# Splitting the first F tiles of a fused S5-scan and MLP kernel by token parity, with zeroed warm-up matmuls and later waits for weights

## The chip, the cores and the metric

The kernel runs on one core of one Trainium2 chip. The metric is the device time of one launch in microseconds (us). The engines are named as the profile names them: PE (TensorE, matmuls; PEld is its weight load), DVE (VectorE), ACT (ScalarE), POOL (GpSimd) and SP (SyncE, which here only issues DMAs). Each engine works through its own queue in order, and engines wait for one another by semaphores.

## What is computed

The input is x with 2048 tokens of 448 values. It is normalised, and two things are made of the normalised xn: a diagonal complex state-space scan (S5) and a gated two-layer MLP. In short:

```python
xn = layernorm(x)
Lam_bar = exp(dt * Lam);  B_bar = ((Lam_bar - 1) / Lam)[:, None] * Bmat
h[t] = Lam_bar * h[t-1] + xn[t] @ B_bar.T            # 448 complex states
s = 2 * real(h @ Cmat.T) + xn * Dskip
m = gelu(layernorm(xn) @ w1 + b1) @ w2 + b2          # w1: 448 x 1792, w2: 1792 x 448
out = x + s * silu(m)
```

## The kernel before, in words

Tokens are taken in four groups of 512 (`g`), each of two blocks of 256 tokens (`b`). Two neighbouring tokens share a partition, so that a block is 128 partitions by two token parities (`par`, or `r` in the layout). `xn2T` holds the normalised tokens transposed, with 128 columns for one block and parity.

**The order of the work is written out by hand.** Every operation, or run of operations on one engine, is a task (`Plan.add`, line 64) with the names that it reads and writes. `Plan.link` (line 93) works out which task waits for which. `Plan.emit` (line 112) then goes through the list `ORDER` (line 161) and issues each task on its engine, with all its waits ahead of its first instruction. The tasks are numbered in the order in which the code makes them; a few have names (W0 to W3, B0 to B3, H10, H12 and so on). `SECOND` (line 181) lists the tasks that go to their second choice of engine. An engine never overtakes: a task whose wait isn't met holds up all that stand behind it on that engine.

**The head.** The first block is normalised parity by parity (`first_norm`, line 386): statistics on DVE (393, 394), the root on ACT (395, 396), the scaling on DVE (398, tasks 92 and 99), four transposes on PE (401, tasks 93 and 100), and a copy back from PSUM on DVE (405, tasks 95 and 102). After each four transposes stand five dummy matmuls (403, tasks 94 and 101). Ahead of all that, task 88 (line 828) has PE run 28 dummy matmuls of the identity with itself, which need the identity that POOL makes. Task 45 (lines 480 to 485) is nine tiny matmuls that turn the rows of scan parameters into columns; ACT copies them out (46, the last parameter row for the skip in 47), takes an exponential (48, 54), and POOL computes with them (53, 49 to 52, 55, 56), until ACT takes the absolute value of an angle (task 57, line 512) and POOL goes on with a sine (58).

**The first layer for group 0** (`mm1_half`, line 742) takes 128 x 2 tokens at a time. For each of the seven pairs `j` of F tiles it runs 8 matmuls of 128 weights columns by 256 tokens (both parities at once, 4 slices of D by 2 tiles) into a pair of PSUM banks, and then one gelu on ACT (line 754). The pairs of banks are taken in turn, 0 and 1, 2 and 3, 4 and 5, so the matmuls of a pair wait for the gelu of three pairs earlier. For block 0 the matmul tasks are 114, 116, 118, 120, 122, 124 and 126, and their gelus 115, 117, 119, 121, 123, 125 and 127; for block 1 they are 128 to 141. Task 112 (line 464) is the eight transposes of block 1, and 113 (line 470) their copy. Each first-layer task waits for its chunk of w1: rows 0 to 383 (`w1_c`), the last 64 rows (`w1r_c`), and the row of b1 that stands below them (`w1b`).

**The second layer** (`mm2`, line 758) is 14 matmuls of 128x448 for 128 tokens. The four tasks of group 0 (275, 272, 281, 278) each wait for all four chunks of w2. Then PE goes on with the first layer of group 1 (`mm1`, line 720: an `own` task of 8 matmuls, which has the name H1j, and an `other` task of 6 for each `j`, bank pairs 0 and 1, 2 and 3, 5 and 6), whose gelus on ACT (line 738) are 365 for j = 0, 369 for j = 2, 367 for j = 1. H15 (j = 5) takes the banks that H12 (j = 2) used, so it waits for gelu task 369.

**ACT between the gelus of groups 0 and 1.** ACT multiplies the B matrices, which a DMA brings, by parameters (167 and 169, line 595), copies rows of w1 (W1, W2, W3, line 843; W0 is on DVE, line 844), loads another function table (581), makes the sines and cosines for the scan (579, tasks 162 to 166), takes three silus (766), loads the gelu table again, and goes on with 365. `ln_apply` for the scan's normalised tokens of block 0 is tasks 146 and 147 (one a parity), of block 1 148 and 149; on ACT they are line 449, on DVE line 448. W1 waits for W0.

## Time and profile before

| what | value |
|---|---|
| median of 3 runs | 155.54 us (155.49 to 155.61) |
| the profiled execution's own time | 155.18 us |
| its span, first to last instruction | 153.1 us |
| PE busy | 148.4 us, 97% of the span |
| DVE, ACT, POOL busy | 131.3, 102.5 and 47.3 us |
| granted TensorE clock | 1.000 |

The span is what the profile sees; 2.1 us of the profiled execution's own time lie around it. Busy time counts instructions from their start to their end, and since matmuls overlap in the PE's pipeline, a matmul's duration is longer than the distance to the next one. A row of a timeline gives start, length, engine, line, operation, what is written and read, and how many instructions were merged; a bracket tells the idle time just ahead and what ended it. "q" after an engine is its sequencer, as when SP issues a DMA.

### The profile page before, as it was taken

What the parts mean: (1) busy time and instruction counts of PE and PEld (TensorE: products, weight loads), DVE (VectorE), ACT (ScalarE), POOL (GpSimd) and SP (SyncE); (2) the same over time, 40 slices, a digit from 0 to 9 for tenths busy, and PEclk for the clock granted to TensorE, in tenths of its full rate; (3) what the DMA queues carried; (4) which work ended last, traced back from release to release, by engine and by line L of the source; (5) the groups of instructions that cost most, each with busy time, mean ns of one, the idle gap of its engine ahead of it and who ended that gap; (6) DMA issues with size and microseconds to landing.
All of it is one profiled execution on the core that took longest, in us unless ns stands there. A gap on an engine that the chain in (4) does not pass through costs nothing.

```text
span 153.1 us, 3017 instructions
## 1 busy us (share of the span) xinstructions
PE 148.4 (97%) x1079; PEld 89.9 (59%) x1079; DVE 131.3 (86%) x275; ACT 102.5 (67%) x175; POOL 47.3 (31%) x122
## 2 busy tenths in 40 slices
PE   6999999999999999999999999999999999999992
PEld 6899945454575555755544556665555665555551
DVE  5879999999988999999859998349699539999784
ACT  3876959999885688798993599841419987244110
POOL 6465896374520004700000079000512920000001
PEclk9999999999999999999999999999999999999999
DMA  4998999996859553000003310042300100010103
GB/s 115 311 259 268 349 175 238 211 187 130 160 88 175 88 103 69 0 2 0 4 1 59 84 40 0 0 96 84 62 2 0 62 0 4 0 62 0 60 0 120
DMA packets 31512, 14.04 MB, mean 92 GB/s; under 512 B 25733, under 2 KB 31113, under 8 KB 31498
## 3 DMA queue, kind: packets, MB, share of 16 engines
q1 hardware_dynamic: 31344, 13.80, 39.5%
q8 instruction: 8, 0.13, 0.4%
q10 hardware_dynamic: 154, 0.06, 0.1%
q14 instruction: 6, 0.05, 0.1%
HBM read 6.20 MB, written 1.84 MB: 53 GB/s over the span
## 4 chain that ended last, share of the span: by engine, by line
PE 85%; SPq 6%; DMA 5%; issue 1%; DVE 1%
PE psum L762 28%; PE psum L728 22%; PE psum L654 15%; PE psum L792 13%; SPq L90 6%; DMA w_sb<-in_B_w_dram 5%; PE psum L795 4%; PE psum L636 3%; PE psum L798 1%; PE psum L642 1%; DVE t L801 0%; DVE tmp L804 0%; PE psum L638 0%; PE psum L644 0%
## 5 line engine op out<-in xcount | busy, mean ns | idle before, releaser
L762 PE MATMUL psum<-w_sb,gT 128*128 128x448 bf16 x224 | 44.3, 353 | 0.1
L728 PE MATMUL psum<-xn2T,w_sb 64*128 64x512 bf16 x294 | 33.9, 378 | 0.0
L762 PEld LDWEIGHTS psum<-w_sb,gT 128*128 128x128 bf16 x224 | 21.8, 98 | 19.8 <-DMA w_sb<-in_B_w_dram 0.4
L738 ACT ACTIVATE gT<-psum,b1f 128x512 bf16<-128x512 f32 x42 | 26.0, 687 | 6.9 <-PE psum L728 6.7
L728 PEld LDWEIGHTS psum<-xn2T,w_sb 64*128 64x128 bf16 x294 | 15.6, 109 | 16.1 <-issue 3.0
L654 PE MATMUL psum<-xnT,BT 128*128 128x256 bf16 x196 | 24.1, 273 | 0.0
L654 PEld LDWEIGHTS psum<-xnT,BT 128*128 128x128 bf16 x196 | 18.4, 98 | 6.5 <-issue 3.3
L766 ACT ACTIVATE g_sb<-o 128x448 bf16<-128x448 f32 x16 | 9.1, 572 | 12.2 <-DVE o L765 12.1
L801 DVE TENSOR_TENSOR t<-psum,g_sb 128x448 bf16<-128x448 f32 (+2 forms) x17 | 10.0, 591 | 5.9 <-PE psum L795 2.8
L679 DVE TENSOR_TENSOR_SCAN s_f<-cw,cur,v_sb 128x256 f32<-128x256 f32 x21 | 14.9, 737 | 0.1
L693 POOL TENSOR_TENSOR cwk<-s_f,ang 128x3 f32<-128x3 f32 x3 | 1.4, 470 | 43.3 <-DVE s_f L679 43.3
L748 PE MATMUL psum<-xn2T,w_sb 128*128 128x256 bf16 x112 | 12.6, 273 | 0.3 <-DVE xn2T L405 0.3
L748 PEld LDWEIGHTS psum<-xn2T,w_sb 128*128 128x128 bf16 x112 | 11.9, 111 | 0.7 <-issue 0.4
L792 PE MATMUL psum<-CZ,h_sb 128*128 128x448 bf16 x56 | 11.9, 353 | 0.0
L765 DVE TENSOR_TENSOR o<-psum,b2bc 128x448 f32<-128x448 f32 x16 | 9.7, 614 | 1.7 <-PE psum L762 1.7
L792 PE MATMUL psum<-CQ,h_sb 128*128 128x448 bf16 (+2 forms) x54 | 10.5, 332 | 0.0
L683 ACT ACTIVATE s_b<-s_f 128x1536 bf16<-128x1536 f32 x4 | 5.9, 1485 | 6.7 <-DVE s_f L679 6.7
L658 ACT ACTIVATE u_sb<-psum 128x512 bf16<-128x512 f32 x12 | 7.2, 598 | 4.6 <-PE psum L654 4.6
L448 DVE TENSOR_SCALAR xn_sb<-x_all,lnw 128x448 bf16<-128x448 bf16 (+1 forms) x30 | 9.9, 364 | 0.3
L754 ACT ACTIVATE gT<-psum 128x512 bf16<-128x512 f32 x14 | 8.2, 592 | 2.7 <-PE psum L748 2.7
L804 POOL TENSOR_TENSOR tmp<-t,xr 128x192 bf16<-128x192 bf16 x1 | 0.5, 548 | 26.3 <-DVE t L801 26.3
L792 PEld LDWEIGHTS psum<-CZ,h_sb 128*128 128x128 bf16 x56 | 5.3, 98 | 5.1 <-issue 0.5
(160 smaller groups left out, 236.9 us busy)
## 6 DMA issues: line engine op xcount, KB each, us to landing
out_dram<-tmp SPq DMA_DIRECT2D x7, 224.0 KB, 1.9
x_all<-in_A_x_dram SPq DMA_DIRECT2D x3, 448.0 KB, 4.7
w_sb<-in_B_w_dram SPq DMA_DIRECT2D x3, 448.0 KB, 7.3
w_sb<-in_B_w_dram SPq DMA_DIRECT2D x3, 384.0 KB, 4.4
Bn<-in_A_B_im_dram SPq DMA_DIRECT2D x1, 336.0 KB, 8.5
Bn<-in_A_B_re_dram SPq DMA_DIRECT2D x1, 336.0 KB, 8.7
x_all<-in_A_x_dram SPq DMA_DIRECT2D x2, 112.0 KB, 2.1
x_all<-in_A_x_dram SPq DMA_DIRECT2D x1, 224.0 KB, 2.7
```

The source lines that it names most:

```text
L90: return e.dma_start(out_ap, in_ap)
L448: on = [("dve", [lambda e, o=o, i=i: e.tensor_scalar(o, i, rs, nb, op0=ALU.mult, op1=ALU.add) for o, i in pairs], 0.4, 0.12), ("act", [lam ...
L654: fns = [lambda e, r=r, m=m, d=d: e.matmul(psum[:, 4, r * NK:(r + 1) * NK], BT[:, m, d, :], xnT[:, gx, d, :], start=(d == 0), stop=(d == 6 ...
L679: dve(lambda e, i=i, ri=ri, init=init: e.tensor_tensor_scan(s_f[:, i, ri, :], col(R2, i).to_broadcast([128, NK]), v_sb[:, i, ri, :], init, ...
L728: return lambda e: e.matmul(psum[:, b0 + k, :], w1_sb[halves[h], d, fcol(2 * j + k)], rhs[halves[h], d, :, :], start=first and d == 0, sto ...
L738: act([lambda e, k=k: e.activation(gT[:, gb, 2 * j + k, :], psum[:, b0 + k, :], ACT.Gelu_apprx_tanh, bias=b1f[:, 2 * j + k:2 * j + k + 1]) ...
L748: fns = [lambda e, k=k, d=d: e.matmul(psum[:, banks[k], :].rearrange("p (r c) -> p r c", r=2)[:, :, cs], w1_sb[:, d, fcol(2 * j + k)], rhs ...
L762: fns = [lambda e, fi=fi: e.matmul(psum[:, bk, 0:D], gT[:, gb, fi, q * 128:(q + 1) * 128], w2_sb[:, fi, :], start=(fi == 0), stop=(fi == N ...
L765: dve(lambda e: e.tensor_tensor(o2[:, ob, :], psum[:, bk, 0:D], b2bc[:], ALU.add), [f"ps{bk}", "b2bc"], [f"oo{ob}"], 0.62, prio - 76)
L766: act(lambda e: e.activation(g_sb[:, gs, :], o2[:, ob, :], ACT.Silu), [f"oo{ob}"] + (["silu"] if g == 0 else []), [f"g{gs}"], 0.58, prio - ...
L792: fns = [lambda e, k=k: e.matmul(psum[:, bk, c0:c1], h_sb[:, hb, k, k0:k0 + 128], cm[:, k, c0:c1], start=(k == 0), stop=False) for k in ra ...
L801: dve(lambda e: e.tensor_tensor(t3[:, fb, c0:c1], psum[:, bk, c0:c1], g_sb[:, gs, c0:c1], ALU.mult), [f"ps{bk}", f"g{gs}"], [f"t3{fb}_{c0} ...
```

## The change

- **First F tiles by parity.** For block 0, the pairs j = 0 and j = 1 become two tasks of 16 matmuls of 128 tokens each: the first (number 114) does both pairs for parity 0 and waits only for that parity's transposed tokens, the second (115) the same for parity 1. They write banks 0 to 3. The two gelus are then 116 (j = 0) and 117 (j = 1), and both need 115. A new field `behind` takes out the second task's wait for the first.
- **Late waits.** A task can hold waits for an instruction inside it (`late`). First-layer tasks of group 0 wait for the last rows of w1 at their seventh matmul; their loops also change places (slice of D outside, tile inside). Second-layer tasks of group 0 wait for the w2 chunks at matmuls 0, 4, 8 and 12.
- **Dummies.** A new tile `still` of 128x128 is zeroed by DVE (task ST, DVE's first). Task 88 becomes 9 matmuls of 128x512 on `still` in place of 28 of 128x128 on the identity. The dummies after the transposes write bank 4 in place of bank 3.
- **The end.** Of the last three output DMAs, the one for the second half of the last parity's columns goes from ACT's queue to SP's, and the one for the first half from SP's to ACT's.
- **Order.** The head's tasks are reordered, and task 147 goes from ACT to DVE (it leaves `SECOND`).

```diff
+            for i, keys in t.late.items():
+                t.ldeps[i] = {last[k] for k in keys}
+                for k in keys:
+                    readers.setdefault(k, []).append(t)
...
             for k, fn in enumerate(t.ins):
+                need = {}
+                for d in t.ldeps.get(k, ()) if k else t.deps - {t.behind}:
+                    sem, val = done[d]
...
+            kb.tag = "ST"
+            dve(lambda e: e.memset(still[:], 0.0), [], ["still"], 0.1, S0)
...
+            LATE = ((1, 4), (2, 8), (3, 12))
...
+                def part(k, d, r, i=j):
+                    return lambda e: e.matmul(psum[:, (0, 2, 4)[(7 * b + i) % 3] + k, :].rearrange("p (r c) -> p r c", r=2)[:, r, cs],
+                                              w1_sb[:, d, fcol(2 * i + k)], rhs[:, d, r, :], start=(d == 0), stop=(d == 3))
+
+                if b == 0 and j == 0:
+                    for r in range(2):
+                        pe([part(k, d, slice(r, r + 1), i) for i in range(2) for d in range(4) for k in range(2)], [f"xmT0p{r}"] + wk, [f"ps{k}" for k in range(4)], 0.89, prio)
+                        kb.tasks[-1].late = {6: ["w1r_0"]}
+                    kb.tasks[-1].behind = kb.tasks[-2]
+                elif b or j > 1:
+                    pe([part(k, d, slice(0, 2)) for d in range(4) for k in range(2)], (["xmT0p0", "xmT0p1"] if b == 0 else ["xmT0_1"]) + wk, [f"ps{k}" for k in banks], 0.89, prio)
+                    kb.tasks[-1].late = {6: [f"w1r_{chunk[2 * j]}"]}
...
-                pe(fns, [f"gT{gb}_{fi}_{b}" for fi in range(NF)] + [f"w2_{c}" for c in range(4)], [f"ps{bk}"], 2.66, prio)
+                pe(fns, [f"gT{gb}_{fi}_{b}" for fi in range(NF)] + [f"w2_{c}" for c in range(1 if g == 0 else 4)], [f"ps{bk}"], 2.66, prio)
+                if g == 0:
+                    kb.tasks[-1].late = {w: [f"w2_{c}"] for c, w in LATE}
...
-                        kb.dma("act" if c0 else "sp", dram_ap(out, off + par * D + c0, [[2 * D, 128], [1, w]]), o_sb[:, ob, par * D + c0:par * D + c1], reads=[f"o{ob}_{par}_{c0}"],
+                        kb.dma("act" if par and not c0 else "sp", dram_ap(out, off + par * D + c0, [[2 * D, 128], [1, w]]), o_sb[:, ob, par * D + c0:par * D + c1], reads=[f"o{ob}_{par}_{c0}"],
...
-            pe([lambda e: e.matmul(psum[:, 3, 0:128], ident[:, :], ident[:, :], start=True, stop=True) for _ in range(28)],
-               ["ident"], ["ps3"], 2.8, 3 * PINNED)
+            pe([lambda e: e.matmul(psum[:, 3, :], still[:, :], still[:, None, :].to_broadcast([128, 4, 128]), start=True, stop=True) for _ in range(9)],
+               ["still"], ["ps3"], 2.8, 3 * PINNED)
```

The lists `ORDER` before and after, taken apart by engine, differ as follows (from where they differ to where they are the same again; numbers as in the code of each):

```
PE before    88 45 93 94 100 101 114 116 118 120 122 112 126 124 128 132 134 130 138 140 136 275
PE after     88 93 94 45 100 101 114 115 118 120 122 124 112 126 128 132 134 130 138 136 140 275
ACT before   98 46 47 48 103 54 115 57 117 119 121 123 127 125 129 149 133 135 131 146 139 147 137 167 141 169 W1 162
ACT after    98 46 48 103 54 116 47 57 117 119 121 123 127 129 125 133 131 135 149 137 139 167 146 141 169 W1 162
POOL before  6 63 53 49 50 51 52 64 65 55 56 58 104 60 DH 69 59 67 312 68 BF 61 62 72 70
POOL after   6 53 49 50 63 64 52 51 55 56 65 58 DH 60 59 69 61 104 312 62 67 72 68 70 (BF after 288)
DVE before   102 106 108 105 107 109 110 144 111 113 305 154 304 148 152 66 306 307 310 308 309 311 155 153 156 157 159 158 160 161 316 317 313 314 W0 168 276
DVE after    102 106 105 108 107 109 110 144 148 111 113 307 304 66 305 311 306 309 310 308 154 153 152 155 156 157 160 158 159 316 317 313 314 161 W0 168 147 276
SP           the transpose 318 goes ahead of the load 195; the rest is as before
```

In these, 161 is the absolute value of the scan's angles (line 571), 312 the scale for group 1's normalisation (POOL, line 422 and on), 316, 317, 313 and 314 that normalisation itself (line 448), and 304 to 311 its statistics. DVE's task 10, the memset of w1's padding (line 309), stood first on DVE and now follows ST.

## The prediction

> **What bounds the kernel now.** I read the page's first and fourth parts, then the chain of work in order of time.
>
> ```profile
> span 153.1 us, 3017 instructions
> ...
> PE 85%; SPq 6%; DMA 5%; issue 1%; DVE 1%
> ```
>
> ```profile
> 11.23 8.32 DMA w_sb<-in_B_w_dram
> ...
> 19.60 10.77 PE psum L762 x56
> ```
>
> The chain is SP issuing loads, then the last w2 chunk landing at 19.55 (11.23 + 8.32), then PE without a break from 19.60 to the tail. So the time is "when does PE begin its second layer" plus a PE stream of fixed length, as long as no other engine holds PE up later. The change touches the first part; the second part is where I look for what it costs. PE's head, from the timeline:
>
> ```profile
> 1.42 3.17 PE L828 MATMUL psum<-ident 128*128 128x128 bf16 x28 [1.42 <-POOL mhalf L314]
> 4.52 0.23 PE L480 MATMUL psum<-ident,vrows 4*128 4x4 bf16 x3
> ...
> 5.01 0.40 PE L401 MATMUL psum<-ident,xn_sb 128*128 128x128 bf16 x4
> ...
> 5.54 0.40 PE L401 MATMUL psum<-ident,xn_sb 128*128 128x128 bf16 x4
> 5.77 0.44 PE L403 MATMUL psum<-ident 128*128 128x128 bf16 x5
> 6.50 4.53 PE L748 MATMUL psum<-xn2T,w_sb 128*128 128x256 bf16 x40 [0.28 <-DVE xn2T L405]
> 10.99 0.62 PE L464 MATMUL psum<-ident,xn_sb 128*128 128x128 bf16 x8
> 11.45 8.03 PE L748 MATMUL psum<-xn2T,w_sb 128*128 128x256 bf16 x72
> 19.60 4.71 PE L762 MATMUL psum<-w_sb,gT 128*128 128x448 bf16 x24
> ```
>
> ```profile
> L748 PE MATMUL psum<-xn2T,w_sb 128*128 128x256 bf16 x112 | 12.6, 273 | 0.3 <-DVE xn2T L405 0.3
> ```
>
> ```profile
> L828 PE MATMUL psum<-ident 128*128 128x128 bf16 x6 | 0.8, 314 | 0.0
> ```
>
> The last two rows, from the page's groups and from the groups between 4.0 and 6.4, have the mean length of one matmul in ns behind the bar. A matmul outlasts the distance to the next, so I take distances: a row's length less one matmul, over its count less one. L748: (4.53 - 0.27)/39 = 0.109 us. L828: (3.17 - 0.31)/27 = 0.106. L464 fills 10.99 to 11.45 with 8: 0.057, twice the pace of L828 for the same shape. PE has that pace from 5.54 (4 in 0.23): it speeds up somewhere between 4.3 and 5.5, at most 4.1 us after its first dummy. All 112 first-layer matmuls plus 8 transposes run nearly without a gap from 6.50; the last could be followed at 19.32, and 0.28 is lost until 19.60.
>
> **The change, part by part.** *Dummies and parameters.* DVE's rows price the new memset:
>
> ```profile
> 1.04 0.81 DVE L309 MEMSET w_sb<- 64x896 uint32 x1 [1.04 <-PEq L906]
> 1.94 0.17 DVE L310 MEMSET xn_sb<- 128x128 uint32 x1
> ...
> 5.45 0.94 DVE L405 COPY xn2T<-psum 128x512 bf16<-128x512 bf16 x2
> ...
> 11.65 0.69 DVE L470 COPY xn2T<-psum 128x1024 bf16<-128x1024 bf16 x1 [0.72 <-PE psum L464]
> ```
>
> (0.81 - 0.17)/768 words is 0.8 ns a word, so `still` (64 words) takes 0.12: 1.04 to 1.16, and with 0.05 for the handover PE starts at 1.21, not 1.42. Nine dummies of 512 columns take 9 x 4 x 0.106 = 3.82 at the slow pace, ending at 5.03; if PE speeds up on the way, at the earliest 2.9 us after its start (4.3 less 1.42), at 4.62. I take 4.95, near the first, since a late end is what the row shows. The first transposes (4 x 0.057), their dummies (5 x 0.057) and the parameter matmuls follow. Task 45 took from 4.38 (end of the dummies at 0.106) to 5.01, 0.63, mostly at the slow pace; at the fast one it lies between 0.32 (half) and 0.63, and I take 0.5. So parity 1's transposes come at 4.95 + 0.51 + 0.5 = 5.96, not 5.54, and the first tile task, behind them and five dummies (9 x 0.057), at 6.47, not 6.50. Parity 0's copy is not the limit: it ends at 5.87 (5.45 + 0.42). **Here the gain is nearly eaten by moving task 45 into the way.** The late wait for w1's last rows takes nothing out: before, the copy came last.
>
> *Half-width tiles.* 32 matmuls of 128 columns replace 16 of 256, each with its own weight load.
>
> ```profile
> L748 PEld LDWEIGHTS psum<-xn2T,w_sb 128*128 128x128 bf16 x112 | 11.9, 111 | 0.7 <-issue 0.4
> L464 PEld LDWEIGHTS psum<-ident,xn_sb 128*128 128x128 bf16 x8 | 0.4, 97 | 0.2 <-DVE xn_sb L448 0.2
> ```
>
> A load of w1 lasts 111 ns against L464's 97 ns. L464's transposes, new weights each, still went at 0.057, so the loads overlap there: 32 x 0.057 = 1.82 against 16 x 0.109 = 1.74. The far end, no overlap, is 32 x 0.111 = 3.55. I take 1.82, the nearest row. Task 118 then starts at 8.29 (before: 8.24), and 122 could at 10.03 (before: 9.99).
>
> The Trainium skill, "TensorE: Matmul & The Clock Gate", Back-to-back issue gap, speaks against this: in a real stream of load and matmul pairs it gives some 81 ns for 128 columns, not 56. By it the estimate for the 32 is 2.59 us; the transposes here, 57 ns apart, don't show it, but their weights lie differently.
>
> *ACT's queue.* Task 122 reuses the banks of j = 1 and waits for gelu 117, which stands on ACT behind task 57.
>
> ```profile
> 8.72 0.21 ACT L512 ACTIVATE ang<-ang 128x16 f32<-128x16 f32 x1 [0.55 <-POOL ang L502]
> 8.84 1.07 ACT L754 ACTIVATE gT<-psum 128x512 bf16<-128x512 f32 x2
> ```
>
> ```profile
> 6.21 0.20 POOL L494 TENSOR_TENSOR ang<-cw 128x4 f32<-128x4 f32 x1
> 6.50 0.23 POOL L495 TENSOR_SCALAR cw<-ang 128x4 f32<-128x4 f32 x1
> 6.70 0.22 POOL L496 TENSOR_SCALAR ang<-ang 128x4 f32<-128x4 f32 x1
> ```
>
> Task 57 waits for POOL, which waits for task 45. Task 45 ends 5.96 - 5.01 = 0.95 later. POOL's new order puts independent operations next to each other (0.20 apart, where dependent ones are 0.29), worth at most 0.2. So gelu 117, which ended at 9.44 (8.84 + 0.60), ends at about 10.2, and 122 starts there: a new stall of 0.17. From there 16 x 0.109 (122, 124), the transposes, and block 1. Moving 124 ahead of 112 drops the gap before L464 (6.50 + 40 x 0.109 = 10.86, started at 10.99), but the copy then lies beside 126 alone: 10.99 to 12.34 and a handover of 0.07 is 1.42, against 0.46 + 0.87 of work. So 10.2 + 1.74 + 1.42 + 56 x 0.109 = 19.46. The w2 waits no longer bind: the first chunks are long there and the last is wanted two microseconds later. **The second layer starts at 19.46 instead of 19.60: 0.14 gained.**
>
> *ACT further on.* This decides. ACT's timeline, the busy times of all engines in one stretch (ACT's is the fourth), the group of group 1's gelus, two pairs of them, and PE's weight loads:
>
> ```profile
> 17.39 0.75 ACT L449 ACTIVATE xn_sb<-x_all,lnw 128x448 bf16<-128x448 bf16 x1
> 18.04 0.58 ACT L754 ACTIVATE gT<-psum 128x512 bf16<-128x512 f32 x1
> 18.52 0.76 ACT L449 ACTIVATE xn_sb<-x_all,lnw 128x448 bf16<-128x448 bf16 x1
> ...
> 21.60 0.67 ACT L595 ACTIVATE tmp<-Bn,cw 128x448 f32<-128x448 bf16 x1 [1.49 <-DMA Bn<-in_A_B_re_dram]
> ```
>
> ```profile
> 21.60:33.00 11.40, 11.40 (x73) 5.83 (x73) 11.08 (x27) 11.16 (x16) 6.57 (x17) 1.00 1.07 222
> ```
>
> ```profile
> L738 ACT ACTIVATE gT<-psum,b1f 128x512 bf16<-128x512 f32 x42 | 26.0, 687 | 6.9 <-PE psum L728 6.7
> ```
>
> ```profile
> 33.05 1.26 ACT L738 ACTIVATE gT<-psum,b1f 128x512 bf16<-128x512 f32 x2
> ```
>
> ```profile
> 34.43 2.42 ACT L738 ACTIVATE gT<-psum,b1f 128x512 bf16<-128x512 f32 x4
> ```
>
> ```profile
> 35.75 1.87 PEld L728 LDWEIGHTS psum<-xn2T,w_sb 64*128 64x128 bf16 x20 [0.33 <-ACT gT L738]
> ```
>
> Before, ACT did tasks 146 and 147 (L449, 17.39 and 18.52) in good time, and then sat idle 1.49 until B landed. From 21.60 to 33.00 it was busy 11.16 of 11.40 (the rest is between instructions): no slack. Its second pair of gelus, at 34.43, released PE's H15 at 35.75. In the new order 167, which waits for B, stands ahead of 146. SP issues B's loads as before, so B lands as before (SP's swap of 318 and 195 comes after them). So 146 leaves the idle time and goes into the full stretch: 0.65 there (17.39 to 18.04). That 147 has left ACT saves only idle time. The first pair of gelus then starts at 33.70, not 33.05, the second at 33.70 + 2 x 0.58 = 34.86 (0.58 = (2.42 - 0.69)/3), and its second half ends at 34.86 + 0.58 + 0.69 = 36.13. H15 starts at 36.18, **0.43 later**, whether or not PE came 0.14 earlier: the head's gain vanishes in this wait. H13, eight matmuls before, waits first, for 33.70 + 1.26 = 34.96.
>
> Could DVE make it worse? W1 on ACT waits for W0 on DVE, now behind task 161.
>
> ```profile
> 18.59 1.23 DVE L571 SCALAR_TENSOR_TENSOR s_f<-s_f 128x1024 f32<-128x1024 f32 x1
> 19.96 2.40 DVE L448 TENSOR_SCALAR xn_sb<-x_all,lnw 128x448 bf16<-128x448 bf16 x8
> 22.40 0.29 DVE L844 COPY w_sb<-w_sb 64x512 bf16<-64x512 bf16 x1
> 23.98 0.61 DVE L765 TENSOR_TENSOR o<-psum,b2bc 128x448 f32<-128x448 f32 x1
> ```
>
> If the normalisation keeps its start at 19.96, W0 ends at 22.69 + 1.23 = 23.92 and W1 is wanted at 23.98: just covered. If it starts up to 0.3 later, ACT slips by as much again. That is the upper bound, 0.7. Task 147 on DVE is one operation of 448 columns, as in the eight of that row. The split output DMAs only swap queues: nothing.
>
> The sum: 153.1 + 0.43 in the span, 155.18 + 0.43 = 155.61 for a profiled execution. The median of before lies 0.36 above its profiled one, so the forecast is 155.54 + 0.43 = **155.97**, 0.28% slower, own range 155.75 to 156.3.
>
> **Rivals.** (1) *ACT has room* and the head's gain stays. ACT must have 146 behind it by 21.60, or B must land by 20.95, 0.65 earlier than the row. Then H15 waits no longer than PE takes: -0.14 gives 155.40, which can't be told from no change (0.2%, 0.31 us, is about what a measurement of this kernel can tell). It becomes **faster** if task 45 also takes its low bound, 0.32: 122 then starts at 10.02, the second layer at 19.28, and the time is 155.2; without POOL's stall, 155.05. For it: ACT's idle 1.49 is large. Against: nothing in the order puts 146 into it.
>
> (2) *The weight loads don't overlap.* 32 tiles at 0.111 make 118 start at 10.02, 122 at 11.76, the second layer at 21.0: 156.95; at half of that extra, 0.084, it is 20.15 and 156.1. Against: L464's pace.
>
> With the Trainium skill's 81 ns (same section) 122 starts at 10.81 and the second layer at 20.07, an estimate of 156.0; H15's wait would hide nearly all of it.
>
> (3) *Multiplying zeros doesn't speed PE up.* Then the slow pace lasts some 3.5 us (the middle of 2.9 and 4.1) from the first transposes at 5.03. The 18 transposes and dummies take 1.9 and task 45 0.63, so the first tile task starts at 7.55; 9 of its 32 matmuls are slow, 23 fast, and 118 starts at 9.8 instead of 8.29. The second layer starts 1.5 later than forecast, at about 20.8: 156.75. No row of before shows a matmul of zeros; L828's identity is mostly zeros, and PE sped up all the same.
>
> **How the numbers follow.** Forecast 0.60, rival 1 with no change 0.17 and faster 0.10, rival 2 0.08, rival 3 0.05. About a quarter of the forecast's cases lie under +0.31 (0.14), so slower is 0.46 + 0.08 + 0.05 = 0.59; same is 0.17 + 0.14 = 0.31; faster 0.10. The range 155.3 to 156.4 takes in ACT's upper bound (156.24) and leaves out the faster end and the far ends of rivals 2 and 3.
>
> **What would show it.** In the profile after: first tile task near 6.5, its 32 matmuls 0.057 apart; a PE gap before task 122 with an ACT gelu as releaser; L762 starting near 19.5 with no DMA named; on ACT an L449 between L595 and the gelu after 21.6, gelus for group 1 from 33.7; a PEld wait for L738 of some 0.7 near 36. I am wrong if L738 starts by 33.1, or if L762 starts before 19.2.

## Result and profile after

| | median (us) | lowest to highest | against before |
|---|---|---|---|
| before | 155.54 | 155.49 to 155.61 | |
| after the change | 157.25 | 156.93 to 157.42 | 1.0098, interval 1.0086 to 1.011 |

The change makes the kernel 1% slower: 1.7 us where 0.43 was forecast, and outside the range of the prediction. The profiled execution took 157.34 us, with a span of 155.2 against 153.1. In the new numbering L848 are the dummies, L411 and L413 the transposes and dummies behind them, L490 to L494 the parameters, L761 the tile tasks and L772 their gelus, L474 and L480 block 1's transposes and their copy, L780 the second layer, L785 and L786 its bias and silu, L738 and L748 the first layer of the later groups and its gelus, L458 and L459 normalisations on DVE and ACT, L605, L606 and L608 work on B, L581 the absolute value (task 161), L863 and L864 the copies W1 to W3 and W0, L796 a product on POOL.

PE's timeline of the kernel after, to be laid beside the one in the prediction (start, length, engine, line, operation, count; in brackets the idle time before and what ended it):

```profile
1.04 3.96 PE L848 MATMUL psum<-still 128*128 128x512 bf16 x9 [1.04 <-DVE still L301]
4.89 0.40 PE L411 MATMUL psum<-ident,xn_sb 128*128 128x128 bf16 x4
5.13 0.44 PE L413 MATMUL psum<-ident 128*128 128x128 bf16 x5
...
5.96 0.40 PE L411 MATMUL psum<-ident,xn_sb 128*128 128x128 bf16 x4
6.19 0.44 PE L413 MATMUL psum<-ident 128*128 128x128 bf16 x5
6.47 1.95 PE L761 MATMUL psum<-xn2T,w_sb 128*128 128x128 bf16 x32
8.85 3.65 PE L761 MATMUL psum<-xn2T,w_sb 128*128 128x256 bf16 x32 [0.43 <-DMA w_sb<-in_B_w_dram]
12.34 0.61 PE L474 MATMUL psum<-ident,xn_sb 128*128 128x128 bf16 x8
12.79 7.41 PE L761 MATMUL psum<-xn2T,w_sb 128*128 128x256 bf16 x64
20.04 5.46 PE L780 MATMUL psum<-w_sb,gT 128*128 128x448 bf16 x28
25.86 5.46 PE L780 MATMUL psum<-w_sb,gT 128*128 128x448 bf16 x28 [0.36 <-DVE o L785]
31.25 4.74 PE L738 MATMUL psum<-xn2T,w_sb 64*128 64x512 bf16 x42
36.51 1.05 PE L738 MATMUL psum<-xn2T,w_sb 64*128 64x512 bf16 x8 [0.53 <-ACT gT L748]
37.76 2.35 PE L738 MATMUL psum<-xn2T,w_sb 64*128 64x512 bf16 x20 [0.19 <-ACT gT L748]
```

Before, PE went from 19.60 to the tail without a break; the row behind the second layer was

```profile
30.30 7.80 PE L728 MATMUL psum<-xn2T,w_sb 64*128 64x512 bf16 x70
```

and the next work began at 38.03. Now there is a break in the head, before 8.85, for w1's second chunk, and there are three behind the start of the second layer, each with its releaser in brackets: a bias on DVE before 25.86, a gelu on ACT before 36.51 and again before 37.76. The second layer starts 0.44 later (20.04 against 19.60); the span grew by 2.1. So the greater part, 1.7, is lost after 20 us, far behind the head that the change is about.

This gives a measure that is used below: **the span less the start of the second layer.** It leaves out when PE gets through the head in the one execution that was profiled, though not what the head leaves undone on the other engines. Before it is 153.1 - 19.60 = 133.5, after 155.2 - 20.04 = 135.2.

ACT's timeline of the kernel after, from B's landing to the first gelus of group 1:

```profile
22.01 0.67 ACT L605 ACTIVATE tmp<-Bn,cw 128x448 f32<-128x448 bf16 x1 [1.56 <-DMA Bn<-in_A_B_re_dram]
22.58 0.74 ACT L459 ACTIVATE xn_sb<-x_all,lnw 128x448 bf16<-128x448 bf16 x1
...
24.39 0.63 ACT L863 ACTIVATE w_sb<-w_sb 64x512 bf16<-64x512 bf16 x1
...
32.23 0.56 ACT L786 ACTIVATE g_sb<-o 128x448 bf16<-128x448 f32 x1
33.90 1.28 ACT L748 ACT_TABLE_LOAD   x1 [1.10 <-issue]
35.19 3.00 ACT L748 ACTIVATE gT<-psum,b1f 128x512 bf16<-128x512 f32 x5
```

The L459 of the prediction stands where it said, behind the first L605. But the last silu ends at 32.79 (32.23 + 0.56), and then ACT does nothing for 1.10 before it loads the gelu table. In the kernel before the load followed the silu at once:

```profile
31.18 0.56 ACT L766 ACTIVATE g_sb<-o 128x448 bf16<-128x448 f32 x1
31.75 1.28 ACT L738 ACT_TABLE_LOAD   x1
```

### The profile page after: what moved, and what is told of

It reads as the page before. It is cut to its first block, busy times and chain, and to the rows that moved or that the text cites. A ratio compares the mean times of both kernels' runs of the same rounds, so it can differ in the third digit from the quotient of the medians.

```text
span 155.2 us, 3005 instructions
## 1 busy us (share of the span) xinstructions
PE 149.7 (96%) x1076; PEld 88.5 (57%) x1076; DVE 131.7 (85%) x277; ACT 101.6 (65%) x174; POOL 46.1 (30%) x122
## 3 DMA queue, kind: packets, MB, share of 16 engines
q1 hardware_dynamic: 31344, 13.79, 40.8%
## 4 chain that ended last, share of the span: by engine, by line
PE 81%; DVE 8%; DMA 4%; issue 2%; ACT 2%; SPq 1%
PE psum L780 24%; PE psum L738 19%; PE psum L664 14%; PE psum L812 13%; PE psum L815 4%; DMA w_sb<-in_B_w_dram 4%; PE psum L646 3%; PE psum L761 2%; DVE xn_sb L458 1%; SPq L92 1%; ACT gT L748 1%; DVE lnst L389 1%; DVE s_f L578 1%; PE psum L818 1%; ACT L748 1%
## 5 line engine op out<-in xcount | busy, mean ns | idle before, releaser
L780 PE MATMUL psum<-w_sb,gT 128*128 128x448 bf16 x224 | 44.5, 352 | 0.4 <-DVE o L785 0.4
L738 PE MATMUL psum<-xn2T,w_sb 64*128 64x512 bf16 x294 | 34.3, 378 | 0.7 <-ACT gT L748 0.7
L780 PEld LDWEIGHTS psum<-w_sb,gT 128*128 128x128 bf16 x224 | 21.8, 98 | 20.0 <-ACT w_sb L863 0.8
L748 ACT ACTIVATE gT<-psum,b1f 128x512 bf16<-128x512 f32 x42 | 26.0, 691 | 7.0 <-PE psum L738 6.9
L738 PEld LDWEIGHTS psum<-xn2T,w_sb 64*128 64x128 bf16 x294 | 15.9, 109 | 16.9 <-issue 2.8
L664 PE MATMUL psum<-xnT,BT 128*128 128x256 bf16 x196 | 24.1, 273 | 0.0
L664 PEld LDWEIGHTS psum<-xnT,BT 128*128 128x128 bf16 x196 | 18.4, 98 | 6.5 <-issue 2.9
L786 ACT ACTIVATE g_sb<-o 128x448 bf16<-128x448 f32 x16 | 9.1, 572 | 12.3 <-DVE o L785 12.0
L689 DVE TENSOR_TENSOR_SCAN s_f<-cw,cur,v_sb 128x256 f32<-128x256 f32 x21 | 15.7, 774 | 0.2
L761 PE MATMUL psum<-xn2T,w_sb 128*128 128x256 bf16 (+1 forms) x128 | 13.0, 259 | 0.4 <-DMA w_sb<-in_B_w_dram 0.4
L761 PEld LDWEIGHTS psum<-xn2T,w_sb 128*128 128x128 bf16 x128 | 11.8, 111 | 1.2 <-PE psum L761 0.6
L785 DVE TENSOR_TENSOR o<-psum,b2bc 128x448 f32<-128x448 f32 x16 | 9.7, 612 | 1.7 <-PE psum L780 1.5
L458 DVE TENSOR_SCALAR xn_sb<-x_all,lnw 128x448 bf16<-128x448 bf16 (+1 forms) x31 | 10.2, 363 | 0.1
L772 ACT ACTIVATE gT<-psum 128x512 bf16<-128x512 f32 x14 | 7.8, 593 | 3.8 <-PE psum L761 3.7
L796 POOL TENSOR_TENSOR xr<-xd,g_sb 128x448 f32<-128x448 bf16 x3 | 3.1, 1032 | 17.9 <-DVE s_f L689 13.2
```

The lines of the kernel that those rows point to most:

```text
L458: on = [("dve", [lambda e, o=o, i=i: e.tensor_scalar(o, i, rs, nb, op0=ALU.mult, op1=ALU.add) for o, i in pairs], 0.4, 0.12), ("act", [lam ...
L664: fns = [lambda e, r=r, m=m, d=d: e.matmul(psum[:, 4, r * NK:(r + 1) * NK], BT[:, m, d, :], xnT[:, gx, d, :], start=(d == 0), stop=(d == 6 ...
L689: dve(lambda e, i=i, ri=ri, init=init: e.tensor_tensor_scan(s_f[:, i, ri, :], col(R2, i).to_broadcast([128, NK]), v_sb[:, i, ri, :], init, ...
L738: return lambda e: e.matmul(psum[:, b0 + k, :], w1_sb[halves[h], d, fcol(2 * j + k)], rhs[halves[h], d, :, :], start=first and d == 0, sto ...
L748: act([lambda e, k=k: e.activation(gT[:, gb, 2 * j + k, :], psum[:, b0 + k, :], ACT.Gelu_apprx_tanh, bias=b1f[:, 2 * j + k:2 * j + k + 1]) ...
L761: return lambda e: e.matmul(psum[:, (0, 2, 4)[(7 * b + i) % 3] + k, :].rearrange("p (r c) -> p r c", r=2)[:, r, cs], w1_sb[:, d, fcol(2 * ...
```

## The experiments

Each was measured beside the kernel before on the same chip. Three chips were used, and the median of before was 155.7 on each. The row of after is the result above, so a difference between two rows can hold a difference between chips. The last column is the measure from above, from the profiled execution.

| kernel | ratio to before | interval | second layer starts | span | from there to the end |
|---|---|---|---|---|---|
| before | 1 | | 19.60 | 153.1 | 133.5 |
| after | 1.0098 | 1.0086 to 1.011 | 20.04 | 155.2 | 135.2 |
| pe_wait_first | 1.0021 | 0.9994 to 1.0048 | 20.21 | 154.4 | 134.2 |
| before_pe_wait_last | 1.0077 | 1.0048 to 1.0105 | 21.07 | 155.8 | 134.7 |
| bias_first | 1.0033 | 1.0002 to 1.0065 | 20.20 | 154.2 | 134.0 |
| norm_first | 1.0081 | 1.005 to 1.0111 | 20.03 | 155.3 | 135.3 |
| old_order | 0.9999 | 0.998 to 1.0018 | 19.73 | 153.5 | 133.8 |
| three | 1.0014 | 0.9998 to 1.0031 | 20.48 | 154.4 | 133.9 |
| abs_first | 1.0067 | 1.0036 to 1.0098 | 19.84 | 154.5 | 134.7 |
| late_alone | 1.0017 | 1.0 to 1.0035 | 19.71 | 153.7 | 134.0 |
| transposes_back | 1.0039 | 1.002 to 1.0057 | 20.38 | 154.1 | 133.7 |
| head_back | 1.0016 | 0.9993 to 1.0039 | 19.65 | 153.5 | 133.9 |
| norm_late | 1.0062 | 1.0039 to 1.0086 | 19.96 | 154.6 | 134.6 |
| b_early | 0.9974 | 0.9957 to 0.9992 | 20.45 | 154.2 | 133.8 |

### The hole on ACT: which wait is written first

Task 365, the first gelus of group 1, waits for several engines at once. The emitter walks through a Python set of tasks, collects one count per semaphore, and issues one wait for each in the order in which the set gave them. What follows calls this reading theory W: the first of these waits rides on the gelu instruction itself; every further one is an instruction of its own, and the table load, which is put in directly ahead of the gelu, stands behind those. In the kernel before, PE's wait came first; in the kernel after, the wait for ACT's own count did, so PE's wait stands ahead of the load. Two kernels test it; they change the order of the waits and nothing else, and each engine keeps the same instructions in the same order.

```diff
 after -> pe_wait_first
-                for sem, val in need.items():
+                for sem, val in sorted(need.items(), key=lambda n: n[0] != "pe") if "gT1_0_0" in t.writes else need.items():
 before -> before_pe_wait_last
-            for sem, val in need.items():
+            for sem, val in sorted(need.items(), key=lambda n: n[0] == "pe") if "gT1_0_0" in t.writes else need.items():
```

> The changed kernel, with one line altered: of the waits of task 365 (ACT's first group-1 gelus) the wait for PE is written first. Every engine has the same instructions in the same order; only the wait for PE moves from a separate instruction ahead of ACT's table load to the gelu behind it. Theory W (the table load of 1.28 us is held up by the wait for PE's task 364, which ends at about 33.8): the load starts as soon as ACT's last silu ends, at 32.8, the gelus start at 34.1 instead of 35.19, H13 and H15 come about 1 us earlier: 157.25 - 1.06 = 156.2. Theory A (the prediction's: task 146 in ACT's full stretch sets the gelus' start): the load is late because ACT is late, nothing changes: 157.25.

> The kernel before, with the same line altered the other way round: the wait of task 365 for PE is written last. Same instructions in the same order. Theory W: the table load waits for task 364, which ends 2.6 us after H10's start at 30.30, so at 32.9; gelus from 34.2 instead of 33.05, H15 at 34.2 + 2.57 = 36.8 instead of 35.75: 155.54 + 1.06 = 156.6, about 0.7% slower without any other difference. Theory A: 155.54, as ACT is as full as it was.

Both came out as theory W had it. The ratio of the changed kernel falls from 1.0098 to 1.0021, that of the kernel before rises from 1 to 1.0077: 1.2 us each way, where 1.06 was expected; the intervals leave some 0.4 on either side. ACT's timeline of pe_wait_first:

```profile
32.20 0.56 ACT L786 ACTIVATE g_sb<-o 128x448 bf16<-128x448 f32 x1
32.78 1.28 ACT L748 ACT_TABLE_LOAD   x1
34.08 1.26 ACT L748 ACTIVATE gT<-psum,b1f 128x512 bf16<-128x512 f32 x2
35.55 1.84 ACT L748 ACTIVATE gT<-psum,b1f 128x512 bf16<-128x512 f32 x3 [0.21 <-PE psum L738]
```

and of before_pe_wait_last:

```profile
32.62 0.56 ACT L766 ACTIVATE g_sb<-o 128x448 bf16<-128x448 f32 x1
34.42 1.28 ACT L738 ACT_TABLE_LOAD   x1 [1.24 <-PE psum L728]
35.71 1.84 ACT L738 ACTIVATE gT<-psum,b1f 128x512 bf16<-128x512 f32 x3
```

In the first the load follows the silu at once, the gelus come at 34.08 instead of 35.19, and now ACT waits for PE (0.21) instead of PE for ACT. PE runs through the 70 matmuls without a break:

```profile
31.43 7.89 PE L738 MATMUL psum<-xn2T,w_sb 64*128 64x512 bf16 x70
```

In the second the hole of 1.24 appears in the kernel before, this time with PE's L728 named as its releaser, and PE then waits for the gelu as it does in the kernel after:

```profile
37.03 3.29 PE L728 MATMUL psum<-xn2T,w_sb 64*128 64x512 bf16 x26 [0.54 <-ACT gT L738]
```

The table load needs nothing from PE. It takes 1.28 us, and it is hidden as long as it runs while PE still works on task 364. Behind PE's wait it isn't, and the gelus come 1.1 later.

The Trainium skill, "ScalarE: Activation LUTs", What ACT_TABLE_LOAD costs, gives some 1283 ns for the load and about as much again for a drain, 2.66 us for a switch. The load agrees (1.28). The drain is not in this trace: from the silu's end at 32.76 to the gelu's start at 34.08 the whole switch takes 1.32.

### ACT's task 146, the step that carried the prediction

```diff
 after -> norm_first   (ORDER)
-... 140 137 139 62 ... 73 146 161 ...
+... 140 146 137 139 62 ... 73 161 ...
```

> The changed kernel with ACT's task 146 moved back ahead of 137, 139 and 167, into the idle time before B lands. Theory A (the prediction's step, 0.65 us in ACT's full stretch): silus end 0.65 earlier and so do the gelus, 0.43 to 0.65 faster: 156.6 to 156.8. Theory W: the last silu ends 0.6 earlier, but the table load still waits for PE until 33.8, so the gelus start at 35.2 as before: 157.25, at most 0.1 away.

1.0081, interval 1.005 to 1.0111, against 1.0098. The two intervals overlap, and alone they are too wide to rule out theory A's 0.43 to 0.65 us. The trace does: the gelus start at 35.26, against 35.19 in after. ACT's timeline of norm_first says why:

```profile
24.22 0.63 ACT L863 ACTIVATE w_sb<-w_sb 64x512 bf16<-64x512 bf16 x1 [0.39 <-DVE w_sb L864]
...
32.06 0.56 ACT L786 ACTIVATE g_sb<-o 128x448 bf16<-128x448 f32 x1
33.97 1.28 ACT L748 ACT_TABLE_LOAD   x1 [1.34 <-PE psum L738]
```

The last silu ends only 0.17 earlier (32.62 against 32.79), because W1 now waits 0.39 for W0 on DVE (24.22 against 24.39), and the load waits for PE as before. The step was tried again where the load doesn't wait for PE and W0 hides only 0.29 us of it: in old_order, below, with both normalisations moved.

```diff
 old_order -> norm_late   (ACT's order)
-... 146 139 147 137 167 141 ...
+... 139 137 167 146 147 141 ...
```

> The kernel old_order (all of the change's code, order of before) with ACT's tasks 146 and 147 moved behind 167, that is out of the idle time before B lands into ACT's stretch after it: twice the dose of the prediction's step, since the change itself moved one of them. ACT had 0.29 us of slack there in old_order (before W1, which waits for DVE). The prediction's step: 1.3 - 0.29 = 1.0 later for the gelus, 33.5 becomes 34.5, H13 and H15 wait 0.7 to 0.9: ratio 1.0045 to 1.006. Rival: DVE or PE sets the gelus' use anyway and nothing is seen: ratio 1.000.

1.0062 against 0.9999 for old_order: 0.0063 of 155.7 is 1.0 us. The gelus come 1.17 later (34.68 against 33.51), 1.44 of work behind B less 0.29 of slack. PE's timeline of norm_late shows one of its two waits directly:

```profile
31.41 8.10 PE L738 MATMUL psum<-xn2T,w_sb 64*128 64x512 bf16 x70 [0.56 <-ACT w_sb L863]
```

It is W3 (L863) that PE waits for here, 0.6 of the 0.8 by which the last column of the table exceeds old_order's; the gelus account for the rest at most. So the first half of the prediction's mechanism exists: a normalisation moved behind B makes ACT late by its length less the slack, and PE pays. That PE pays at the gelus holds for the smaller part. In the kernel after, all this was covered.

### DVE's queue and the stall before task 281

PE's second tile pair at 25.86 waits for bank 6, which task 276 (a bias, L785) frees. DVE's timeline of the kernel after, from the copy of block 1's transposes on:

```profile
12.99 0.69 DVE L480 COPY xn2T<-psum 128x1024 bf16<-128x1024 bf16 x1 [1.41 <-PE psum L474]
...
18.00 1.67 DVE L578 SCALAR_TENSOR_TENSOR s_f<-iota,cw,s_f 128x256 f32<-128x256 f32 x4
19.59 2.40 DVE L458 TENSOR_SCALAR xn_sb<-x_all,lnw 128x448 bf16<-128x448 bf16 x8
21.90 1.22 DVE L581 SCALAR_TENSOR_TENSOR s_f<-s_f 128x1024 f32<-128x1024 f32 x1
23.14 1.01 DVE L864 COPY w_sb<-w_sb 64x512 bf16<-64x512 bf16 x1
...
25.10 0.61 DVE L785 TENSOR_TENSOR o<-psum,b2bc 128x448 f32<-128x448 f32 x1
```

Before, the copy started at 11.65 and the bias at 23.98. Now it is 12.99 and 25.10. Three theories were tried: the order just ahead of the bias, the place of task 161, and the copy.

```diff
 after -> bias_first   (ORDER)
-... W0 71 75 168 W1 147 76 315 276 287 ...
+... W0 71 75 276 168 W1 147 76 315 287 ...
```

> The changed kernel with DVE's task 276 (the bias of the second tile, which frees bank 6 for PE's task 281) one place ahead of 168 and 147. Theory D (DVE's order, 147 and W0 and 168 ahead of 276, holds PE up before 281): the stall of 0.5 us before 281 goes, H10 starts 0.5 earlier, and, since the gelus' table load waits for PE, everything after comes 0.5 earlier: 156.75. Rival: DVE's later work (168 comes 0.6 later) holds PE up further on by as much, or ACT alone sets the gelus' start: 157.25.

The ratio was 1.0033, 1.0 us better than after, but this run doesn't measure what it was made for. The stall before 281 was gone; so was the hole on ACT, though only DVE's order had been edited:

```profile
32.82 1.28 ACT L748 ACT_TABLE_LOAD   x1
34.12 3.06 ACT L748 ACTIVATE gT<-psum,b1f 128x512 bf16<-128x512 f32 x5
```

The order of the waits had come out the other way by itself. A set of objects has no order that the program text fixes; that is the reading of the code that goes with it, and norm_first, where also only ORDER was edited, kept the hole. It makes bias_first a repaired kernel with two changes, and it means that the hole is an accident of the emitter rather than of any edit in the change. From here on every kernel writes PE's wait first. bias_first then compares with pe_wait_first: 134.0 against 134.2, 1.0033 against 1.0021. Of its gain at 281 (H10 starts at 30.89, not 31.43) 0.3 is lost again up to L664, which starts 8.13 behind H10 (39.02) and not 7.82 (39.25). The loss lies ahead of H12, whose first matmul comes at 32.07, behind the end of the next bias at 31.92: moving one bias forward leaves DVE as late as it was.

```diff
 after, PE's wait first -> abs_first   (ORDER)
-... 62 316 67 275 ... 73 146 161 74 ...
+... 62 161 316 67 275 ... 73 146 74 ...
```

> The changed kernel with the wait for PE first at task 365 and DVE's task 161 moved back ahead of 316, as before the change. Theory D: DVE's bias 276 was late by 1.1 us for two reasons, task 147 (0.4) and W0, which took 1.0 instead of 0.29 beside a POOL operation (L796, 22.8 to 24.0). With 161 in its old place W0 comes right behind the normalisation, at about 22.3, ahead of that operation, and takes 0.3; 276 starts by 24.2 and PE does not wait before 281: 0.5 faster than with the wait alone, 155.8. Rival: W0 is long wherever it stands, or 161 pushes the normalisation and 276 back as much: no change from the wait alone, 156.3.

A miss: 1.0067, and the bias came at 25.28, as in pe_wait_first. (PE's idle time before 281 grew from 0.37 to 0.74 because its second layer started 0.37 earlier, at 19.84.) In DVE's timeline of abs_first W0 starts no earlier than in after (23.14) and is no shorter:

```profile
23.16 1.18 DVE L864 COPY w_sb<-w_sb 64x512 bf16<-64x512 bf16 x1
...
25.28 0.61 DVE L785 TENSOR_TENSOR o<-psum,b2bc 128x448 f32<-128x448 f32 x1
```

The rival holds: 161 pushes the normalisation back as much as it came forward itself. Besides, POOL's eight L529 beside it now last 2.76 instead of 1.79, and ACT's first L605 waits for them until 22.34. DVE isn't late because of the place of 161; in after it was late before that, by 160's end (19.67 against 18.56 in the kernel before, 18.00 + 1.67 for the one). That leads to the copy, behind which all of this queues, and so to PE's task 124, 8 matmuls (0.87) that the change puts ahead of the transposes.

```diff
 after, PE's wait first -> transposes_back   (ORDER)
-... 121 110 144 124 39 148 123 111 40 112 41 126 ...
+... 121 110 144 39 148 123 111 40 112 41 126 124 ...
 transposes_back -> head_back   (ORDER, besides)
-... 92 98 30 93 94 99 31 45 95 ...  140 137 139 ...  146 161
+... 92 98 30 45 93 94 99 31 95 ...  140 146 137 139 ...  161
```

> The changed kernel with task 365's wait for PE first and, on PE alone, task 124 moved back behind 126, so that block 1's transposes (112) come 0.87 us earlier. Theory T: DVE's whole queue hangs on the copy of these transposes (task 113), which ended 1.34 later than before the change, 0.87 of it by 124; with 124 back the copy ends at about 12.7 to 13.0 (for a first tile task at 6.5 to 6.9), task 160 near 18.8, task 276 starts near 24.2 instead of 25.1, and PE no longer waits before 281 (or by at most 0.1). 0.4 to 0.5 us faster than with the wait alone: ratio 0.998 to 1.000. Rival: DVE is held by 147 or by W0 beside POOL's L796, the copy was not on its path: 276 stays at 25 and the ratio at 1.002.

> As transposes_back, and further task 45 (parameters) back ahead of 93 on PE and task 146 ahead of 137 on ACT; the rest of the change's order stays. Theory: gelu 117 no longer waits behind task 57, so the stall of 0.17 before task 122 goes, DVE and ACT are about as early as before: ratio 0.997 to 0.999. Rival: the tasks 45 ahead of parity 0's transposes delay the first tile task as much as they did behind them, and 0.17 is lost in a later wait: as transposes_back.

In transposes_back the copy started at 12.58, task 160 ended at 19.27, and the normalisation, W0 and the bias came 0.3 to 0.4 earlier than after's:

```profile
12.58 0.69 DVE L480 COPY xn2T<-psum 128x1024 bf16<-128x1024 bf16 x1 [0.72 <-PE psum L474]
...
24.80 0.61 DVE L785 TENSOR_TENSOR o<-psum,b2bc 128x448 f32<-128x448 f32 x1
```

PE has no break before 281:

```profile
11.93 0.62 PE L474 MATMUL psum<-ident,xn_sb 128*128 128x128 bf16 x8 [0.47 <-DVE xn_sb L458]
...
20.38 10.76 PE L780 MATMUL psum<-w_sb,gT 128*128 128x448 bf16 x56
```

From the second layer on it needs 133.7 against pe_wait_first's 134.2, the 0.5 that theory T asked for. But DVE isn't what got ahead. The whole head ran earlier in this execution: parity 1's transposes came at 6.20, not at 6.54, and counted from them the copy starts only 0.24 sooner (6.38 behind them, not 6.62). What the edit moved is PE. From the copy's start to the bias DVE takes 12.1 to 12.2 us in both runs; to the second layer PE takes 7.05 in pe_wait_first (13.16 to 20.21) and 7.80 here. So with 124 behind the transposes PE comes to 281 some 0.75 later after the copy, and finds the bias done.

The median shows no gain, 1.0039 against 1.0021 with intervals that overlap, and PE's first row says where it went: the transposes now stand in front of a wait of 0.47 for the normalised x of block 1, which DVE delivers late. Task 124 had filled that wait. head_back has the same 0.46 there, starts its second layer at 19.65 and is at 1.0016. So 124's move is an exchange: about 0.5 gained in the head, 0.5 lost at 281.

three puts the repairs of the tail together in the change's own order.

```diff
 after, PE's wait first -> three   (ORDER)
-... 140 137 139 ... 73 146 161 ... 75 168 W1 147 76 315 276 287
+... 140 146 137 139 ... 73 161 ... 75 276 168 W1 147 76 315 287
```

> The changed kernel with three repairs together: the wait for PE first at task 365, task 276 ahead of 168 on DVE, task 146 ahead of 137 on ACT. Theory: the first gives 1.06 us, the second at most 0.5 of which DVE takes some back before H12 (its task 282 frees bank 6 late), the third nothing as long as the gelus do not hold PE up: ratio 1.000 to 1.003, and no wait of PE for a gelu in 31 to 38. The prediction's step (146 in ACT's full stretch sets the gelus): the third gives 0.4 more than the other two: ratio 0.998.

1.0014, within the first theory; no wait for a gelu is left. 146's return gives nothing that can be seen, as norm_first said.

### The code without the order, and one part alone

```diff
 after, PE's wait first -> old_order
-ORDER, SECOND of after
+ORDER, SECOND of before (114 and 115 the two split tasks, ST ahead of all)

 before -> late_alone
-                pe(fns, [f"gT{gb}_{fi}_{b}" for fi in range(NF)] + [f"w2_{c}" for c in range(4)], [f"ps{bk}"], 2.66, prio)
+                pe(fns, [f"gT{gb}_{fi}_{b}" for fi in range(NF)] + [f"w2_{c}" for c in range(1 if g == 0 else 4)], [f"ps{bk}"], 2.66, prio)
+                if g == 0:
+                    kb.tasks[-1].late = {w: [f"w2_{c}"] for c, w in ((1, 4), (2, 8), (3, 12))}
 with Task, link and emit as in after
```

> All of the change's code (split first tiles, zero dummies, late waits for w1's last rows and w2) under the order of before on every engine, with task 365's wait for PE written first. Theory: everything that was lost lay in the order and in that wait, the code itself gains the wait for the last w2 chunk (0.28 us in the profile of before, more where it lands late) and a little in the head: L780 starts at 19.3 to 19.5, gelus at 33.0, time 0.1 to 0.4 us under before, a ratio of 0.997 to 0.9995. Rival: the code costs too (split tiles, late waits as separate instructions): ratio 1.003 or more. Rival 2: ACT's full stretch up to 33.0 takes the head's gain back: H15 waits for a gelu at 35.75 as before, ratio 1.000.

> The kernel before with one part of the change alone: the second layer's first tasks wait for w2's chunks 1 to 3 only ahead of the matmul that reads them (task 365's wait for PE first, as in before). Theory: PE waited 0.28 us for the last chunk in the profile of before; that goes, and more in executions in which the chunk lands later: 155.3 to 155.5 against 155.6 to 155.7, ratio 0.997 to 0.999. Rival: H15 waits for ACT's gelus at 35.75 whenever PE comes earlier, so nothing is gained: ratio 1.000.

old_order is at 0.9999, late_alone at 1.0017: the split tiles, the zero dummies and the late waits neither cost nor give anything that these runs can tell from none. The expected 0.1 to 0.4 us didn't come. By its ratio the second rival fits, that a later limit takes them back; but old_order's profile has no earlier second layer to take back (19.73, after a wait for w1's second chunk until 8.73), so the limit stays open. b_early tries one candidate, the landing of B.

```diff
 old_order -> b_early   (SP's order)
-... 38 39 40 41 36 34 37 35 43 ...
+... 38 39 40 36 34 41 37 35 43 ...
```

> The kernel old_order with SP issuing the two large loads of B ahead of w2's last chunk. With the late waits that chunk is read only 2.3 us after the second layer starts, so its 0.8 us of transfer can come behind B. Theory: B lands 0.8 earlier (20.7 instead of 21.5), the last chunk near 21.5, just before it is read, ACT's stretch up to the gelus starts earlier by 0.8 less what PE's last tile tasks and W0 on DVE hold up, the gelus start up to 0.5 earlier and the head's gain of the late waits reaches the end: ratio 0.996 to 0.998, faster than both kernels. Rival: DVE's chain (normalisation at 20 to 22.4, then W0) is what ACT waits for, or the last chunk now lands too late: ratio 1.000 to 1.003.

0.9974, interval 0.9957 to 0.9992: **0.4 us faster than the kernel before**, the only one of twelve whose interval lies below 1, and by a narrow margin. In its profile B's first landing released nothing any more:

```profile
21.56 0.67 ACT L605 ACTIVATE tmp<-Bn,cw 128x448 f32<-128x448 bf16 x1 [0.31 <-POOL cw L532]
...
24.53 0.63 ACT L863 ACTIVATE w_sb<-w_sb 64x512 bf16<-64x512 bf16 x1 [1.26 <-DVE w_sb L864]
```

ACT waits for POOL and then 1.26 for DVE's W0 instead of for B. That the earlier B is the cause of the gain is not shown. The profiled execution took 155.94, the longest of this kernel's, with its first tile task only at 7.13; in it the gelus come 13.79 behind the start of the second layer (34.24 - 20.45), as in old_order (33.51 - 19.73 = 13.78); and the interval overlaps with old_order's.

## Why the prediction was wrong

**The head was right.** Dummies end near 4.9 (forecast 4.95), parity 1's transposes at 5.96 (5.96), the first tile task at 6.47 (6.47). That they agree to the hundredth is luck: with the same head the first tile task came at 7.21 in pe_wait_first and at 7.34 in three. The 32 half tiles are 0.056 apart ((1.95 - 0.2)/31; forecast 0.057), so rivals 2 and 3 are out: weight loads overlap, and zeros speed PE up. (The prediction's "at most 4.1 us" for the speed-up was loose: the first transposes of before already go at the fast pace, 4 from 5.01 to 5.25. Only the price of rival 3 hung on it.) With the 81 ns that the prediction took from the Trainium skill, task 118 could not have started before 9.06; the last of the 32 ended at 8.42. The stall of 0.17 before task 122, for the gelu behind task 57, is in norm_first's trace with that size; in after's a longer wait came first and swallowed it.

**w1's second chunk: not priced.** Task 118 waited until 8.85 instead of starting at 8.29. The chunk was issued at 3.26 as before and landed 5.45 later, at 8.71:

```profile
3.26 5.45 DMA w_sb<-in_B_w_dram
```

It isn't an effect of the change: the median from issue to landing of these three loads was 4.4 before and 5.5 after, but 4.5 in pe_wait_first and 4.6 in norm_first, whose heads are the same as after's. B varied in the same way. "B lands as before" fails by 0.4 in the profiled execution (22.01 against 21.60), and that too is a matter of the execution.

**"ACT further on", the deciding step, named the wrong thing.** It had the gelus at 33.70 by 0.65 of task 146; they came at 35.19. Of the 1.49 between, B's later landing is 0.4 and the table load behind PE's wait 1.1 (34.08 to 35.19). ACT's stretch from the first L605 to the end of the last silu did grow by 0.64 (22.01 to 32.79, against 21.60 to 31.74), as forecast; but only 0.17 of that is 146's own, since without it ACT waits for W0 until nearly the same moment. Nor is the 0.4 all B's: in pe_wait_first ACT began at 21.76, waited 0.24 for W0 and had its gelus at 34.08 all the same. The waits of PE that the prediction named, H13 and H15 for the first gelus, are there (0.53 and 0.19); the reason that it gave for them is not. The prediction had the row of the first gelus at 33.05 and didn't ask what stood between them and the last silu: a table load of 1.28, which had been hidden beside task 364 and could come out. The cover was the term to price, not ACT's share of busy time.

**"DVE just covered" looked at the wrong customer.** W0 was examined for ACT, at the 0.29 that it took before; it took 1.01 and ended at 24.15, not at 23.92. The bias behind it, which frees a bank for PE, was not examined. And "moving 124 ahead of 112 drops the gap before L464" counted what PE gains in the head and not what it meets afterwards: DVE comes from the copy to task 276 no sooner, and PE waits for it before 281. That took back 0.5.

**The sum, as measured.** In the measure from the second layer's start: 135.2 - 134.2 = 1.0 for the table load, 134.2 - 133.7 = 0.5 for the wait for DVE's bias, 0.2 (133.7 against 133.5) unexplained. PE's rows of after give the same two without a second run: the second layer took 11.21 (20.04 to 31.25, against 10.70 before), the 70 matmuls behind it 8.79 (31.25 to 40.04, against 30.30 to 38.03, 7.73). In medians: about 1.2 of the 1.7 us is the load; the other 0.5 contains the DVE term and what the head gives or takes, and can't be split further with intervals of 0.2 to 0.3%. Slower was right; the size and the cause were not, and the reason given was covered by two others.

## What to carry to other kernels

When a step is priced, look at what stands between the last work of an engine and its next: a table load that is hidden beside another engine's work comes onto the path as soon as the wait for that work is put ahead of it, so it matters which of several waits is written first. A scheduler that walks through an unordered set leaves that to chance; fix the order of the waits, here the one that ends last first, before any orders of tasks are compared. And when work is moved ahead of an operation to fill a gap, ask what the engine will meet when it is done sooner: a queue on another engine that hasn't moved gives the gain back as a wait.

## What the hardware showed besides

**When PE speeds up varies by about 3 us between the profiled executions.** In after's profile the first transposes already go at the fast pace (4 matmuls from 4.89 to 5.13); in pe_wait_first, with the same head, they are at the slow pace until 6.9, and the first tile task comes 0.74 later:

```profile
4.99 0.58 PE L411 MATMUL psum<-ident,xn_sb 128*128 128x128 bf16 x4
5.37 0.74 PE L413 MATMUL psum<-ident 128*128 128x128 bf16 x5
...
6.54 0.55 PE L411 MATMUL psum<-ident,xn_sb 128*128 128x128 bf16 x4
6.93 0.44 PE L413 MATMUL psum<-ident 128*128 128x128 bf16 x5
7.21 0.50 PE L761 MATMUL psum<-xn2T,w_sb 128*128 128x128 bf16 x6
```

From one row's start to the next, the first four transposes take 0.38 here, and the five dummies 0.67 the first time and 0.28 the second. The Trainium skill, "TensorE: Matmul & The Clock Gate", What's actually happening, has a free-running window of 3413 ns that doesn't begin with the kernel, and a transition that varies by 500 ns either way. The spread here is larger, from 3.7 us after the start (old_order, where the eighth of the zeroed dummies follows the seventh by 0.29, and the ninth the eighth by 0.21, instead of 0.43) to 6.9 us; the 3.2 between them would fit into such a window. No order of the head that was tried removes it, and with the same head the first tile task comes up to 0.9 us later (6.47 in after, 7.34 in three, where a wait for DVE adds to it).

**A copy on DVE can wait for POOL while it counts as busy.** W0 (64 x 512) took 0.29 us in the kernel before and 1.01 in after, and in three:

```profile
23.59 1.01 DVE L864 COPY w_sb<-w_sb 64x512 bf16<-64x512 bf16 x1
```

```profile
22.37 2.08 POOL L796 TENSOR_TENSOR xd<-xn_sb,dbc 128x448 bf16<-128x448 bf16 x1
```

W0 ends at 24.60, POOL's product at 24.45; in after 24.15 and 24.01, in abs_first 24.34 and 24.18. It ends 0.14 to 0.16 after POOL's product in all three, whenever it began, and so it does in all eleven profiles in which the product started first, old_order and late_alone with the order of before among them. In the other three (before, before_pe_wait_last, head_back) the product did not start ahead of W0, and W0 took 0.29. The product in turn took 2.08 in three, where it began beside DVE's task 161, and 1.03 in abs_first. The Trainium skill, "SBUF — State Buffer", SBUF: two separate sides, calls this an exclusive lock on a port pair that DVE and POOL share, held for a whole instruction by the one that starts first; the ends above agree. The kernel before may have paid the same toll in another row (its first L598 lasted 1.34 from 22.72 beside POOL's product, the next one 0.67), but there the end lies 0.49 behind the product's, so that is not shown.
